# Attention and a gated feed-forward layer on one core: long-run loads with an on-chip permutation, a new order of loads, stores and transposes, and weight sums on GpSimd

## The chip, the cores and the metric

The kernel runs on one core of one Trainium2 chip. The metric is the device time of one execution in microseconds (us), as a median of several runs; the kernel before takes 463.4 us. Engines in the profile: PE (matmul), PEld (its weight loads), DVE (VectorE), ACT (ScalarE), POOL (GpSimd), SP (SyncE, which here only issues DMAs). Each engine works through its own queue in the order in which the program was emitted. An engine that waits with nothing else to do is said to "stand". A ratio below is the mean time of one kernel's fast runs over that of the kernel before's fast runs of the same rounds on the same chip, so it is not quite the ratio of the medians that stand beside it. The kernel before itself came out at 460 to 465 us on different occasions; so kernels are compared by ratios, and a difference of 0.01 between two ratios is 4.6 us.

## The reference, cut to what matters

```python
# q, k, v: (8 batches, 12 heads, 448 rows, 64);  w_gate, w_val: (768, 1536);  w_out: (1536, 768); all float32
scores = q @ k.T / sqrt(64)
attn   = maximum(scores, 0) ** 2 / 448
x      = heads of (attn @ v) side by side        # 3584 tokens x 768
out    = (maximum(x @ w_gate, 0) * (x @ w_val)) @ w_out
```

The kernel works in bf16 with float32 accumulation. Four heads of one batch make a "quad"; there are 24 quads, three to a batch.

## The kernel before: the parts that matter

The kernel doesn't emit instructions in the order in which it is written. Every operation is an `Op` with a guessed duration per engine; a planner simulates all engines, picks for each operation engine and time, and emits everything in the order of the planned starts. On the chip that order is fixed, right or wrong: if an input is later than planned, the engine stands at that instruction, and all behind it stand too (in the kernel before, DVE stood 10.62 us at one instruction whose weights landed at 104.6 us, and did 0.63 us of work between 92.8 and 104.4).

```python
        op.start, op.eng = s, e
        self.t[e] = s + occ                                    # engine free again
        op.end = s + busy                                      # result there
        if op.load:
            self.dmaq = max(self.dmaq, s + occ + 1.0) + op.load
            op.end = self.dmaq + 1.0                           # guessed landing of a load
        op.end += op.land                                      # the same for transposes and stores
```

Q and k of batches 2 to 7 are loaded in runs of 64 elements straight into the layout that the crossbar wants (`raw`, one buffer), four DMAs a quad, and transposed by DMA, five transposes a quad (a "crossbar group" below):

```python
    src = lambda x: x[b, hs].rearrange("h (p t) d -> p t h d", t=NT)
    ...
    op = Op({"SP": (0.2, 0.2)}, emit, deps=st.qk_ops, alloc=[st.qt_buf], reads=[st.raw_buf])   # five DMA transposes
    op.land = 5.0
```

Batches 2 to 7 use Strassen's scheme for two batches at a time: seven products in place of eight. For that, twelve sums of weights (128x1536 bf16) are formed once, in place, when the plain feed-forward of batches 0 and 1 is done:

```python
    def make_T(after):
        for g in range(KH):
            prev = []
            for o, a, c in (...):                              # four a group, each after the one ahead of it
                op = Op({"DVE": (0.85, 0.97)}, lambda ...: nc.vector.tensor_tensor(
                    o(g), a(g), c(g), ALU.subtract), deps=after + prev)
```

Other two-input work of DVE: the squares (`at*at`), the sums of x (`sx`, `xT`) and of h (`sh`) for Strassen. They read both inputs from SBUF.

Of the kernel before, what the change touches and what calls it, by code (L numbers as in the profile page):

```python
# [53 lines left out]
class Planner:  # L54
    NOUT = 8
    SWITCH = 0.1

    def __init__(self):
        self.t = {}
# [18 lines left out]
    def best(self, op):  # L78
        r = self.ready(op)
        if r is None:  # L80
            return None
        c = None
        for e, (occ, busy) in op.engs.items():
            s = max(r, self.t.get(e, 0.0))
            if e == "PE" and op.mode != self.mode:
                s = max(r, self.t.get(e, 0.0) + self.SWITCH)
            if c is None or s + busy < c[0]:
                c = (s + busy, s, e)
        return c[1], c[2], r

    def commit(self, op, s, e):
        op.start, op.eng = s, e
        occ, busy = op.engs[e]
        self.t[e] = s + occ
        op.end = s + busy
        if e == "PE":
            self.mode = op.mode
        if op.load:
            self.dmaq = max(self.dmaq, s + occ + 1.0) + op.load
            op.end = self.dmaq + 1.0  # L100
            self.landed.append(op.end)
        op.end += op.land
        for b in op.alloc:
            b.idx = b.pick()[1]
            for w in range(b.width):
                del b.res.free[b.idx + w]
            b.last = op.end
        for b in op.reads:
            b.readers -= 1
            b.last = max(b.last, op.end)  # L110
            if b.readers == 0:
                for w in range(b.width):
                    b.res.free[b.idx + w] = b.last
        self.ops.append(op)


def plan(att, ffn, others, pool, deadline):
# [16 lines left out]
    while ai < len(att) or fi < len(ffn) or active or pi < len(pool):  # L134
        cands = []
        for op in active:
            b = P.best(op)
            if b is not None:
                cands.append((b[0], b[2], 1, b[1], op))
        if pi < len(pool):  # L140
            b = P.best(pool[pi])
            if b is not None:
                s = b[0]
                if pi >= P.NOUT:
                    s = max(s, P.landed[pi - P.NOUT])
                cands.append((s, 0.0, 0, "POOL", pool[pi]))
        A = P.best(att[ai][0]) if ai < len(att) else None
        F = P.best(ffn[fi][0]) if fi < len(ffn) else None
        pick = None
        if ai < len(att) and fi < len(ffn) and last_grp is not None and last_grp == ffn[fi][0].grp:  # L150
            pick = "F" if F is not None else None
        elif A is not None and F is not None:
            if att[ai][1] == last_burst:
                pick = "A" if A[0] <= F[0] + 0.4 else "F"
            elif since >= gap:
                pick = "A" if A[0] <= F[0] + 0.15 else "F"
            else:
                pick = "F" if F[0] <= A[0] + 0.3 else "A"
        elif A is not None:
            pick = "A"  # L160
        elif F is not None:
            pick = "F"
        if pick == "A":
            cands.append((A[0], A[2], 2, "PE", att[ai][0]))
        elif pick == "F":
            cands.append((F[0], F[2], 2, "PE", ffn[fi][0]))
        assert cands, f"no operation can start: {ai} {fi} {len(active)} {pi}"
        s, _, kind, e, op = min(cands, key=lambda c: c[:3])
        P.commit(op, s, e)
        for o in outs.get(id(op), ()):  # L170
            o.missing -= 1
            if not o.missing:
                active.append(o)
        if kind == 0:
            pi += 1
        elif kind == 1:
            active.remove(op)
        elif pick == "A":
            if att[ai][1] != last_burst:
                last_burst = att[ai][1]  # L180
                since = 0.0
            ai += 1
            last_grp = None
            sg = ffn[fi][1] if fi < len(ffn) else None
            left = deadline(sg) - last_burst + 1 if sg is not None and deadline(sg) is not None else 0
            gap = left_work[sg] / max(1, left) if left > 0 else 0.0
        else:
            since += op.engs["PE"][0]
            left_work[ffn[fi][1]] -= op.engs["PE"][0]
            last_grp = op.grp  # L190
            fi += 1
# [5 lines left out]
def kernel(  # L197
# [35 lines left out]
    pool = ctx.enter_context(tc.tile_pool(name="sb", bufs=1))  # L233
    psum = ctx.enter_context(tc.tile_pool(name="psum", bufs=1, space=bass.MemoryType.PSUM))

    N_QT, N_AT, N_X, N_F, N_G, N_O = 3, 11, 3, 5, 4, 6
    N_RAW, N_VV = 1, 3

    ps = psum.tile([128, 8, 512], FP32, name="ps")
    ps_b = ps.bitcast(BF16)  # L240
# [4 lines left out]
    wo = pool.tile([128, 2, 2, FH, OH], BF16, name="wo")  # L245
    gvT = pool.tile([128, 3, KH, d_ff], BF16, name="gvT")
    woT = pool.tile([128, 3, FH, OH], BF16, name="woT")
    raw_t = [pool.tile([128, 2, NT, 2, D], BF16, name=f"raw{i}") for i in range(N_RAW)]
    vv_t = [pool.tile([128, 4, NC + 2, D], BF16, name=f"vv{i}") for i in range(N_VV)]
    qkT_t = [pool.tile([128, 2, 2, S], BF16, name=f"qkT{i}") for i in range(N_QT)]  # L250
    at_t = [pool.tile([128, 2, S], BF16, name=f"at{i}") for i in range(N_AT)]
# [6 lines left out]
    o_t = [pool.tile([128, OH], FP32, name=f"o{i}") for i in range(N_O)]  # L258

    r_ps = Res(8)  # L260
    r_raw, r_vv, r_qt, r_at = Res(N_RAW), Res(N_VV), Res(N_QT), Res(N_AT)
    r_x, r_f, r_g, r_o = Res(N_X), Res(N_F), Res(N_G), Res(N_O)
    r_sx, r_sh, r_h = Res(1), [Res(1) for _ in range(4)], Res(1)

# [7 lines left out]
    A384, V384 = (0.40, 0.54), (0.467, 0.61)  # L272
    A896, V896 = (0.83, 0.98), (1.0, 1.13)

    PAIRS = [0, 2]
    SINGLES = [7, 6, 5, 4]

    def bank(among=None):
# [2 lines left out]
    def bank2(among=None):  # L281
        return Buf(r_ps, among if among is not None else PAIRS, width=2)

# [52 lines left out]

    def load_qk(b, g):
        st = quads[(b, g)] = Quad()
        if b < NPE:
            hs = slice(4 * g, 4 * g + 4)  # L340
            st.raw_buf = None
            st.raw = lambda: early_raw(b, g)
            src = lambda x: x[b, hs].rearrange("h (p t) d -> p h t d", t=NT)
            k_op = dma_in(lambda: st.raw()[64:128], src(k), 256, 1.2)
            q_op = dma_in(lambda: st.raw()[0:64], src(q), 256, 1.2)
            st.qk_ops = [k_op, q_op]
        else:
            st.raw_buf = Buf(r_raw)
            st.raw = lambda: raw_t[st.raw_buf.idx]
            st.qk_ops = []  # L350
            for j in range(2):
                hs = slice(4 * g + 2 * j, 4 * g + 2 * j + 2)
                src = lambda x: x[b, hs].rearrange("h (p t) d -> p t h d", t=NT)
                st.qk_ops += [dma_in(lambda j=j: st.raw()[64:128, j], src(k), 896, 0.9,
                                     alloc=[st.raw_buf] if j == 0 else []),
                              dma_in(lambda j=j: st.raw()[0:64, j], src(q), 896, 0.9)]

    def load_v(b, g):
        st = quads[(b, g)]
# [4 lines left out]
        else:  # L364
# [1 line left out]
            st.vv = lambda: vv_t[st.vv_buf.idx]  # L366
        src = v[b, hs].rearrange("h (p t) d -> p h t d", t=NT)
        st.v_of = lambda hh, c: st.vv()[:, hh, 1 + c, :]
        v0 = dma_in(lambda: st.vv()[0:64, :, 1:NC + 2], src[:, :, 0:NC + 1], 256, 0.7,
                    alloc=[st.vv_buf] if st.vv_buf else [])  # L370
        v1 = dma_in(lambda: st.vv()[64:128, :, 0:NC + 1], src[:, :, NC:NT], 256, 0.7)
        st.v_ops = [v0, v1]


    def transpose_pe(b, g):
        st = quads[(b, g)]
        ps2 = bank2()

        def emit():
            raw = st.raw()  # L380
# [27 lines left out]
    def transpose_dma(b, g):  # L408
        st = quads[(b, g)]
        st.qt_buf = Buf(r_qt)  # L410

        def emit():
            raw, qkT = st.raw(), qkT_t[st.qt_buf.idx]
            nc.sync.dma_start_transpose(out=qkT[:, 0].rearrange("p j (t c) -> p (j t) c", c=P2),
                                        in_=raw[0:64].rearrange("p j t h d -> p (j t h d)"))
            for j in range(2):
# [1 line left out]
                for o, t0, t1 in ((0, 0, NC + 1), (1, NC + 1, NT)):  # L418
                    nc.sync.dma_start_transpose(out=kT[:, o:NT:2], in_=raw[64:128, j, t0:t1].rearrange("p t h d -> p (t h d)"))  # L419

        op = Op({"SP": (0.2, 0.2)}, emit, deps=st.qk_ops, alloc=[st.qt_buf], reads=[st.raw_buf])
        op.land = 5.0
        st.qt_ops = [op]
        others.append(op)

    xop, xbuf = {}, {}

    class Attention:
# [11 lines left out]
            return qkT_t[self.st.qt_buf.idx][64 * h2:64 * h2 + 64, 1, j, o:o + n]  # L440

        def s(self, i):
            ps2 = bank2()
            tail = i == 2 * NC
            at = self.at[i] = Buf(r_at)

# [28 lines left out]

        def pv(self):
            b, g, st = self.b, self.g, self.st
            ps2 = bank2()

            def emit_tail():  # L480
                at = at_t[self.at[2 * NC].idx]
# [79 lines left out]
    def make_T(after):  # L561

        res = {}
        for g in range(KH):
            prev = []
            for o, a, c in ((lambda g: gvT[:, 1, g], lambda g: wv[:, 2 * g + 1], lambda g: wv[:, 2 * g]),
                            (lambda g: wv[:, 2 * g], lambda g: wv[:, 2 * g], lambda g: wg[:, 2 * g]),
                            (lambda g: gvT[:, 0, g], lambda g: wv[:, 2 * g + 1], lambda g: wv[:, 2 * g]),
                            (lambda g: gvT[:, 2, g], lambda g: wg[:, 2 * g + 1], lambda g: gvT[:, 0, g])):
                op = Op({"DVE": (0.85, 0.97)}, lambda o=o, a=a, c=c, g=g: nc.vector.tensor_tensor(  # L570
                    o(g), a(g), c(g), ALU.subtract), deps=after + prev)
                others.append(op)
                prev = [op]
# [137 lines left out]
    def store(ob, op, where):  # L711
# [4 lines left out]
            for half, (bb, t) in enumerate(slots):  # L716
                nc.sync.dma_start(out=rows(bb)[t][:, hf * OH:(hf + 1) * OH], in_=o_t[ob.idx][64 * half:64 * half + 64])

        st = Op({"SP": (0.15, 0.15)}, emit, deps=[op], reads=[ob])
        st.land = 2.5  # L720
        others.append(st)

# [91 lines left out]
        load_v(0, g)  # L814
    for c in range(d_ff // WC):
        load_gv(c)
        if c % 2 == 0:
            load_qk(1, c // 2)
            load_v(1, c // 2)
    for g in range(NQ):  # L820
        load_qk(2, g)
        load_v(2, g)
        if g > 0:
            load_out(0, g - 1)
    load_out(1, 0)
    load_out(1, 1)
    for b in range(3, B):
        for g in range(NQ):
            load_qk(b, g)
# [22 lines left out]
    for n, qd in enumerate(A_):  # L852
# [1 line left out]
        att += [(qd.s(0), burst), (qd.s(1), burst)]  # L854
        burst += 1
        att.append((qd.s(2 * NC), burst))
        PV(n - 1)
        T(n + 1)
        burst += 1
        att += [(qd.s(2), burst), (qd.s(3), burst)]  # L860
        burst += 1
        att += [(qd.s(4), burst), (qd.s(5), burst)]
    burst += 1
    PV(len(A_) - 1)

# [45 lines left out]
```

## Time and profile before

| | before |
|---|---|
| median of runs | 463.4 us |
| PE busy, of 464.7 us | 415.1 us |
| DVE busy | 332.8 us |
| feed-forward begins | 43.5 us |
| DVE stands at the output weights | 10.6 us |
| POOL waits for the crossbar to free `raw` | 126.7 us |

PE is the bound on average, and the question is only where its 50 idle microseconds lie and what they wait for. The prediction below shows the lines and reads them.

### The profile page before, as it was taken

How to read it: one execution, taken by the hardware profiler on the slowest of the kernel's cores; microseconds unless marked ns; L12 is line 12 of the kernel's file. 1: busy time of each engine (PE TensorE's matmuls, PEld its weight loads, DVE VectorE, ACT ScalarE, POOL GpSimd, SP SyncE). 2: the span in 40 equal slices, each digit the busy share in tenths (PEclk: the TensorE clock that was granted, in tenths of full speed). 3: DMA queues.
4: the chain of work that ended last, by engine and by line, in shares of the span. 5: the costliest groups of instructions: out<-in, count | busy, mean ns of one | idle time of the engine just before them, and what ended most of it. 6: DMA issues, size and time to landing. Idle time of an engine off the chain costs nothing.

```text
span 464.7 us, 7076 instructions
## 1 busy us (share of the span) xinstructions
PE 415.1 (89%) x2580; PEld 195.2 (42%) x2580; DVE 332.8 (72%) x576; ACT 221.9 (48%) x329; POOL 134.9 (29%) x154
## 2 busy tenths in 40 slices
PE   4768999968988948799999978999999999999994
PEld 2333444423433413244444443444444555555552
DVE  3665877709798833788979967988889686666561
ACT  2564555553574522456555434665654634444221
POOL 7745150605533353145333442253200000000000
PEclk9977999997997968799999999999999999999999
DMA  9999989999857996998669898996721332000144
GB/s 128 196 198 198 151 70 100 108 147 79 82 59 87 122 132 92 128 155 70 74 82 90 85 118 147 167 83 68 72 27 27 76 86 52 1 0 2 34 103 102
DMA packets 138659, 44.13 MB, mean 95 GB/s; under 512 B 103808, under 2 KB 138624, under 8 KB 138624
## 3 DMA queue, kind: packets, MB, share of 16 engines
q0 software_dynamic: 94528, 24.39, 54.5%
q1 hardware_dynamic: 44096, 19.29, 20.9%
q8 instruction: 20, 0.33, 0.3%
q14 instruction: 15, 0.12, 0.1%
HBM read 48.76 MB, written 11.01 MB: 129 GB/s over the span
## 4 chain that ended last, share of the span: by engine, by line
PE 71%; DMA 9%; DVE 7%; SPq 4%; ACT 4%; issue 3%; POOL 1%; DVEq 0%; POOLq 0%; ACTq 0%
PE ps L643 29%; PE ps L744 17%; PE ps L544 8%; PE ps L493 6%; PE ps L451 6%; DMA wo<-in_moe_w_out_dram 4%; SPq L419 3%; DMA out_dram<-o 3%; ACT at L465 3%; PE ps L384 2%; DVE at L467 1%; DMA qkT<-raw 1%; DVE at L470 1%; PE ps L455 1%; PE ps L485 1%
## 5 line engine op out<-in xcount | busy, mean ns | idle before, releaser
L465 ACT ACTIVATE at<-ps 128x896 bf16<-128x896 f32 x117 | 104.4, 918 | 69.2 <-PE ps L451 55.3
L470 DVE TENSOR_TENSOR at<-at 128x896 bf16<-128x896 bf16 x168 | 99.7, 618 | 13.5 <-ACT at L465 13.4
L592 ACT COPY f<-ps 128x448 f32<-128x448 f32 x105 | 55.8, 533 | 66.4 <-PE ps L643 64.5
L288 POOL DMA_DIRECT2D raw<-in_k_dram x36 | 46.2, 1284 | 141.0 <-DMA qkT<-raw 126.7
L467 DVE TENSOR_SCALAR at<-ps 128x896 bf16<-128x896 f32 x51 | 55.3, 1085 | 6.9 <-PE ps L451 6.7
L288 POOL DMA_DIRECT2D raw<-in_q_dram x36 | 59.7, 1662 | 0.3 <-DMA wv<-in_moe_w_val_dram 0.3
L643 PE MATMUL ps<-xT,gvT 128*128 128x448 bf16 x216 | 53.3, 356 | 2.6 <-DVE o L734 2.5
L643 PE MATMUL ps<-sx,wv 128*128 128x448 bf16 x216 | 52.8, 353 | 1.7 <-DVE g L662 1.1
L451 PE MATMUL ps<-qkT 64*128 64x448 bf16 x288 | 45.5, 379 | 9.8 <-ACT at L465 7.1
L643 PE MATMUL ps<-xT,wg 128*128 128x448 bf16 x216 | 52.8, 356 | 0.5 <-DVE g L700 0.5
L288 POOL DMA_DIRECT2D vv<-in_v_dram x44 | 36.4, 1044 | 47.5 <-PE ps L493 40.4
L643 PEld LDWEIGHTS <-gvT 128*128 128x128 bf16 x324 | 31.1, 98 | 37.1 <-issue 9.9
L734 DVE SCALAR_TENSOR_TENSOR o<-ps,f 128x384 f32<-128x384 f32 x40 | 22.0, 554 | 31.1 <-DMA out_dram<-o 16.0
L744 PE MATMUL ps<-wo,hT 128*128 128x384 bf16 x240 | 43.8, 326 | 0.2 <-DVE hT L666 0.2
L744 PEld LDWEIGHTS <-sh 128*128 128x128 bf16 x288 | 27.9, 101 | 36.2 <-issue 10.8
L744 PEld LDWEIGHTS <-hT 128*128 128x128 bf16 x312 | 30.1, 99 | 24.6 <-issue 5.8
L744 PE MATMUL ps<-woT,sh 128*128 128x384 bf16 x144 | 30.1, 359 | 8.4 <-DVE sh L781 8.3
L544 PE MATMUL ps<-xT,wv 128*128 128x448 bf16 x144 | 32.3, 362 | 5.8 <-DVE hT L554 5.8
L493 PE MATMUL ps<-at,vv 128*64 128x448 bf16 x264 | 33.2, 393 | 0.0
L544 PE MATMUL ps<-xT,wg 128*128 128x448 bf16 x144 | 32.6, 364 | 0.0
L594 ACT ACTIVATE f<-ps 128x384 f32<-128x384 f32 x40 | 19.6, 491 | 27.2 <-PE ps L744 26.0
L508 ACT CAST xT<-ps 128x896 bf16<-128x896 f32 x24 | 21.7, 905 | 19.4 <-PE ps L493 19.4
(56 smaller groups left out, 442.1 us busy)
## 6 DMA issues: line engine op xcount, KB each, us to landing
out_dram<-o SPq DMA_DIRECT2D x112, 96.0 KB, 2.9
vv<-in_v_dram POOLq DMA_DIRECT2D x44, 128.0 KB, 5.2
raw<-in_k_dram POOLq DMA_DIRECT2D x36, 112.0 KB, 3.9
raw<-in_q_dram POOLq DMA_DIRECT2D x36, 112.0 KB, 5.0
wg<-in_moe_w_gate_dram POOLq DMA_DIRECT2D x6, 384.0 KB, 11.3
wv<-in_moe_w_val_dram POOLq DMA_DIRECT2D x6, 384.0 KB, 11.2
wo<-in_moe_w_out_dram POOLq DMA_DIRECT2D x4, 576.0 KB, 13.2
qkT<-raw SPq DMA_TRANSPOSE x90, 3.2
```

The source lines that it names most:

```text
L288: op = Op({"POOL": (0.5 + 0.0004 * n_desc,) * 2}, lambda: nc.gpsimd.dma_start(out=dst(), in_=src), deps=deps, alloc=alloc)
L451: nc.tensor.matmul(ps[:, ps2.idx + h2, :S], lhsT=self.k_of(j, h2, c), rhs=self.q_of(j, h2), start=True, stop=True)
L465: nc.scalar.activation(at_t[at.idx], src, AF.Relu)
L467: nc.vector.tensor_scalar_max(at_t[at.idx], src, 0.0)
L470: sq = Op({"DVE": (0.535, 0.66)}, lambda: nc.vector.tensor_tensor(at_t[at.idx], at_t[at.idx], at_t[at.idx], ALU.mult), deps=[relu])
L493: nc.tensor.matmul(ps[o, ps2.idx + j, :S], lhsT=st.v_of(2 * j + h2, c), rhs=at_t[self.at[NC * j + c].idx][:, h2, :], start=False, stop=(c ...
L508: nc.scalar.copy(dst, src)
L544: nc.tensor.matmul(ps[:, pb.idx, :S], lhsT=w[:, kd, fc], rhs=xT_t[xbuf[b].idx][:, kd, :], start=(kd == 0), stop=(kd == KD - 1))
L592: nc.scalar.copy(dst, src)
L643: nc.tensor.matmul(ps[:, pb.idx, :S], lhsT=w(g)[:, fc], rhs=rhs, start=start and g == 0, stop=stop and g == KH - 1, skip_group_check=True)
L734: op = Op({"DVE": V384}, lambda: nc.vector.scalar_tensor_tensor(o_t[ob.idx], ps[:, pb.idx, :OH], float(out_scale), f_t[fb.idx][:, :OH], AL ...
L744: nc.tensor.matmul(ps[:, pb.idx, :OH], lhsT=lhs(kf), rhs=rhs(kf), start=start and kf == 0, stop=kf == FH - 1, skip_group_check=True)
```

## The change

Its intent: longer DMA runs and fewer DMA issues; `raw` freed early by a permutation on chip, so that loads run ahead of the crossbar; a plan that knows what SP's queue really costs; output weights earlier; a denser start; and twelve weight sums taken off busy DVE onto idle GpSimd. The core of the diff, cuts marked "...":

```diff
-            self.dmaq = max(self.dmaq, s + occ + 1.0) + op.load
-            op.end = self.dmaq + 1.0
+            self.dmaq = max(self.dmaq, s + occ + 0.3) + op.load
+            op.end = self.dmaq + 2.0
...
-    N_QT, N_AT, N_X, N_F, N_G, N_O = 3, 11, 3, 5, 4, 6
+    N_QT, N_AT, N_X, N_F, N_G, N_O = 3, 10, 3, 5, 4, 5
...
-    PAIRS = [0, 2]
+    PAIRS, FIRST_PAIRS = [0, 2], [0, 2, 4, 6]            # FIRST_PAIRS: for batch 0
...
+        hs = slice(4 * g, 4 * g + 4)                     # all batches: two DMAs a quad, long runs
+        src = lambda x: x[b, hs].rearrange("h (p t) d -> p h t d", t=NT)
...
+        perm = Op({"DVE": (0.6, 0.72), "ACT": (1.8, 1.95)}, None, deps=st.qk_ops, alloc=[pb], reads=[st.raw_buf])
+        ...      src = st.raw()[:, 2 * j:2 * j + 2].rearrange("p h t d -> p t h d")
+        ...      nc.vector.tensor_copy(dst, src)          # j = 0, 1; dst = perm_t[pb.idx][:, j]
-        op = Op({"SP": (0.2, 0.2)}, emit, deps=st.qk_ops, alloc=[st.qt_buf], reads=[st.raw_buf])
-        op.land = 5.0
+        op = Op({"SP": (6.3, 6.3)}, emit, deps=[perm], alloc=[st.qt_buf], reads=[pb])
+        op.land = 2.6
...
-                op = Op({"DVE": (0.85, 0.97)}, lambda ...: nc.vector.tensor_tensor(
+                op = Op({"POOL": (2.8, 2.9)}, lambda ...: nc.gpsimd.tensor_tensor(
...
-        st = Op({"SP": (0.15, 0.15)}, emit, deps=[op], reads=[ob])      # a pair of stores
+        st = Op({"SP": (1.2, 1.2)}, emit, deps=[op], reads=[ob])
... (guessed load times changed a little; output weights ahead of the second quad of batch 2; q, k, v of batch 1 one weight chunk later;
     the product of quad 2 and the transposes of quad 3 moved ahead of quad 3's scores;
     0.3 us of bias towards ACT where DVE and ACT can both do an operation)
```

More of the change, by code (lines that the diff above doesn't have):

```diff
@@ L56 @@
     SWITCH = 0.1
+    BIAS = 0.3
+    RESERVE = 0.0
     def __init__(self):
@@ L86, in best @@
                 s = max(r, self.t.get(e, 0.0) + self.SWITCH)
-            if c is None or s + busy < c[0]:
-                c = (s + busy, s, e)
+            f = s + busy + (self.BIAS if e == "DVE" and len(op.engs) > 1 else 0.0)
+            if c is None or f < c[0]:
+                c = (f, s, e)
         return c[1], c[2], r
@@ L185, in plan @@
             left = deadline(sg) - last_burst + 1 if sg is not None and deadline(sg) is not None else 0
-            gap = left_work[sg] / max(1, left) if left > 0 else 0.0
+            gap = max(0.0, left_work[sg] - P.RESERVE) / max(1, left) if left > 0 else 0.0
         else:
@@ L234 @@
     psum = ctx.enter_context(tc.tile_pool(name="psum", bufs=1, space=bass.MemoryType.PSUM))
-    N_QT, N_AT, N_X, N_F, N_G, N_O = 3, 11, 3, 5, 4, 6
-    N_RAW, N_VV = 1, 3
+    N_QT, N_AT, N_X, N_F, N_G, N_O = 3, 10, 3, 5, 4, 5
+    N_RAW, N_PERM, N_VV = 1, 1, 3
     ps = psum.tile([128, 8, 512], FP32, name="ps")
@@ L247 @@
     woT = pool.tile([128, 3, FH, OH], BF16, name="woT")
-    raw_t = [pool.tile([128, 2, NT, 2, D], BF16, name=f"raw{i}") for i in range(N_RAW)]
+    raw_t = [pool.tile([128, 4, NT, D], BF16, name=f"raw{i}") for i in range(N_RAW)]
+    perm_t = [pool.tile([128, 2, NT, 2, D], BF16, name=f"perm{i}") for i in range(N_PERM)]
     vv_t = [pool.tile([128, 4, NC + 2, D], BF16, name=f"vv{i}") for i in range(N_VV)]
@@ L260 @@
     r_ps = Res(8)
-    r_raw, r_vv, r_qt, r_at = Res(N_RAW), Res(N_VV), Res(N_QT), Res(N_AT)
+    r_raw, r_perm, r_vv, r_qt, r_at = Res(N_RAW), Res(N_PERM), Res(N_VV), Res(N_QT), Res(N_AT)
     r_x, r_f, r_g, r_o = Res(N_X), Res(N_F), Res(N_G), Res(N_O)
@@ L338, in load_qk @@
         st = quads[(b, g)] = Quad()
-        if b < NPE:
-            hs = slice(4 * g, 4 * g + 4)
-            st.raw_buf = None
-            st.raw = lambda: early_raw(b, g)
-            src = lambda x: x[b, hs].rearrange("h (p t) d -> p h t d", t=NT)
-            k_op = dma_in(lambda: st.raw()[64:128], src(k), 256, 1.2)
-            q_op = dma_in(lambda: st.raw()[0:64], src(q), 256, 1.2)
-            st.qk_ops = [k_op, q_op]
-        else:
-            st.raw_buf = Buf(r_raw)
-            st.raw = lambda: raw_t[st.raw_buf.idx]
-            st.qk_ops = []
-            for j in range(2):
-                hs = slice(4 * g + 2 * j, 4 * g + 2 * j + 2)
-                src = lambda x: x[b, hs].rearrange("h (p t) d -> p t h d", t=NT)
-                st.qk_ops += [dma_in(lambda j=j: st.raw()[64:128, j], src(k), 896, 0.9,
-                                     alloc=[st.raw_buf] if j == 0 else []),
-                              dma_in(lambda j=j: st.raw()[0:64, j], src(q), 896, 0.9)]
+        hs = slice(4 * g, 4 * g + 4)
+        st.raw_buf = None if b < NPE else Buf(r_raw)
+        st.raw = lambda: early_raw(b, g) if b < NPE else raw_t[st.raw_buf.idx]
+        src = lambda x: x[b, hs].rearrange("h (p t) d -> p h t d", t=NT)
+        k_op = dma_in(lambda: st.raw()[64:128], src(k), 256, 1.15, alloc=[st.raw_buf] if b >= NPE else [])
+        q_op = dma_in(lambda: st.raw()[0:64], src(q), 256, 1.15)
+        st.qk_ops = [k_op, q_op]
     def load_v(b, g):
@@ L368, in load_v @@
         st.v_of = lambda hh, c: st.vv()[:, hh, 1 + c, :]
-        v0 = dma_in(lambda: st.vv()[0:64, :, 1:NC + 2], src[:, :, 0:NC + 1], 256, 0.7,
+        v0 = dma_in(lambda: st.vv()[0:64, :, 1:NC + 2], src[:, :, 0:NC + 1], 256, 0.66,
                     alloc=[st.vv_buf] if st.vv_buf else [])
-        v1 = dma_in(lambda: st.vv()[64:128, :, 0:NC + 1], src[:, :, NC:NT], 256, 0.7)
+        v1 = dma_in(lambda: st.vv()[64:128, :, 0:NC + 1], src[:, :, NC:NT], 256, 0.66)
         st.v_ops = [v0, v1]
@@ L376, in transpose_pe @@
         st = quads[(b, g)]
-        ps2 = bank2()
+        ps2 = bank2(FIRST_PAIRS if b == 0 else PAIRS)
         def emit():
@@ L410, in transpose_dma, with emit_perm @@
         st.qt_buf = Buf(r_qt)
+        pb = Buf(r_perm)
+        perm = Op({"DVE": (0.6, 0.72), "ACT": (1.8, 1.95)}, None, deps=st.qk_ops, alloc=[pb], reads=[st.raw_buf])
+        def emit_perm():
+            for j in range(2):
+                dst = perm_t[pb.idx][:, j]
+                src = st.raw()[:, 2 * j:2 * j + 2].rearrange("p h t d -> p t h d")
+                if perm.eng == "ACT":
+                    nc.scalar.copy(dst, src)
+                else:
+                    nc.vector.tensor_copy(dst, src)
+        perm.emit = emit_perm
         def emit():
-            raw, qkT = st.raw(), qkT_t[st.qt_buf.idx]
+            raw, qkT = perm_t[pb.idx], qkT_t[st.qt_buf.idx]
             nc.sync.dma_start_transpose(out=qkT[:, 0].rearrange("p j (t c) -> p (j t) c", c=P2),
@@ L419, in emit @@
                     nc.sync.dma_start_transpose(out=kT[:, o:NT:2], in_=raw[64:128, j, t0:t1].rearrange("p t h d -> p (t h d)"))
-        op = Op({"SP": (0.2, 0.2)}, emit, deps=st.qk_ops, alloc=[st.qt_buf], reads=[st.raw_buf])
-        op.land = 5.0
+        op = Op({"SP": (6.3, 6.3)}, emit, deps=[perm], alloc=[st.qt_buf], reads=[pb])
+        op.land = 2.6
         st.qt_ops = [op]
-        others.append(op)
+        others.extend([perm, op])
     xop, xbuf = {}, {}
@@ L442, in s @@
         def s(self, i):
-            ps2 = bank2()
+            ps2 = bank2(FIRST_PAIRS if self.b == 0 else PAIRS)
             tail = i == 2 * NC
@@ L477, in pv @@
             b, g, st = self.b, self.g, self.st
-            ps2 = bank2()
+            ps2 = bank2(FIRST_PAIRS if b == 0 else PAIRS)
             def emit_tail():
@@ L569, in make_T @@
                             (lambda g: gvT[:, 2, g], lambda g: wg[:, 2 * g + 1], lambda g: gvT[:, 0, g])):
-                op = Op({"DVE": (0.85, 0.97)}, lambda o=o, a=a, c=c, g=g: nc.vector.tensor_tensor(
+                op = Op({"POOL": (2.8, 2.9)}, lambda o=o, a=a, c=c, g=g: nc.gpsimd.tensor_tensor(
                     o(g), a(g), c(g), ALU.subtract), deps=after + prev)
@@ L816 @@
         load_gv(c)
-        if c % 2 == 0:
+        if c % 2 == 1:
             load_qk(1, c // 2)
             load_v(1, c // 2)
-    for g in range(NQ):
-        load_qk(2, g)
-        load_v(2, g)
-        if g > 0:
-            load_out(0, g - 1)
-    load_out(1, 0)
-    load_out(1, 1)
+    load_qk(2, 0)
+    load_v(2, 0)
+    for par in range(2):
+        for hf in range(2):
+            load_out(par, hf)
+        load_qk(2, 1 + par)
+        load_v(2, 1 + par)
     for b in range(3, B):
@@ L856 @@
         att.append((qd.s(2 * NC), burst))
-        PV(n - 1)
-        T(n + 1)
+        if n != NQ:
+            PV(n - 1)
+        if n != NQ - 1:
+            T(n + 1)
         burst += 1
@@ L862 @@
         att += [(qd.s(4), burst), (qd.s(5), burst)]
+        if n == NQ - 1:
+            burst += 1
+            PV(n)
+            T(n + 1)
     burst += 1
```

## The prediction

> **What bounds the kernel now.** I read the page first (busy shares, slices), then the stretches of 11.6 us, then the chain of waits, the waits by engine, and the timelines of PE, DVE, POOL and the DMA queue of SP.
>
> ```profile
> PE 415.1 (89%) x2580; PEld 195.2 (42%) x2580; DVE 332.8 (72%) x576; ACT 221.9 (48%) x329; POOL 134.9 (29%) x154
> ...
> PEclk9977999997997968799999999999999999999999
> ```
>
> PE is the bound on average, yet it is idle for 464.7 - 415.1 = about 50 us, and the low figures of the PEclk row all lie in the first 17 slices (about 197 us). The stretches say where:
>
> ```profile
> 23.20:34.80 11.60, 7.65 (x64) 3.60 (x63) 7.03 (x12) 7.00 (x8) 5.77 (x9) 0.71 1.42 197
> 46.40:58.00 11.60, 11.60 (x99) 5.64 (x98) 10.24 (x16) 6.20 (x8) 2.34 (x3) 1.00 1.42 152
> 92.80:104.40 11.60, 8.00 (x50) 3.39 (x47) 0.63 (x2) 6.33 (x9) 0.00 (x0) 1.00 1.29 149
> 162.40:174.00 11.60, 4.95 (x22) 1.95 (x22) 3.64 (x8) 3.13 (x6) 5.89 (x6) 0.68 0.98 126
> ```
>
> After the window come its length, then PE, PEld, DVE, ACT and POOL busy time, granted clock, DMA share and GB/s. Where attention runs beside the feed-forward part (second row) PE is full. Summing 11.6 minus PE busy over all stretches: 0 to 46 us loses 15.5; 81 to 116 loses 6.5; 127 to 151 loses 3.2; 162 to 197 loses 11.2; 266 to 290 loses 4.2; the drain of the last tiles 5.5; everything else about 3. That is 49. So only about 40 us are up for discussion, four fifths of them ahead of 197 us; from there to 440 us PE is 98% busy and no change off PE can help much.
>
> Each gap has a second price. The timeline shows the same six plain 448-column matmuls at 1.30 us in most of the run and at 2.40 us at 106.6, right after a gap. Clock 0.71 in a stretch is, at half rate while cold, 0.58 x 11.6 = 6.7 cold us, in which work takes double time: up to 3.3 us more per such stretch. Behind the later gaps (104 to 116, 139 to 151, 162 to 197) I estimate 10 to 12 us of this, and before 43 us everything is cold: the 12 matmuls of one attention product take 2.4 us, later 1.26.
>
> The chain and the waits name the causes:
>
> ```profile
> 72.36 1.54 SPq L419
> 73.95 6.16 DMA qkT<-raw
> ...
> 86.59 18.02 DMA wo<-in_moe_w_out_dram
> ...
> 166.37 3.63 DMA out_dram<-o
> ...
> 183.78 3.69 DMA out_dram<-o
> ...
> 275.88 5.08 DMA out_dram<-o
> ```
> ```profile
> POOL raw L288 <- DMA qkT<-raw: 126.7, 19, 16.1
> ...
> DVE o L734 <- DMA out_dram<-o: 16.0, 4, 7.1
> ...
> DVE woT L583 <- DMA wo<-in_moe_w_out_dram: 10.6, 1, 10.6
> ```
>
> (waited us in total, times, longest). First, DVE stands 10.6 us in its queue at the output-weight sum because the last output weights land at 104.6; PE runs out of evicted banks 5.8 us before that ends. Second, stores stand behind transposes in SP's queue: at 159.0 to 165.7 SP issues one crossbar group (five transposes, 1.24 us each, 6.3 in all), the six output tiles fill, DVE waits 7.07 us and PE 6.5; the same at 182 and 273. Third, q and k loads wait for the previous crossbar group, since there is one raw buffer: the groups start at 113.7, 129.1, 143.5, 159.0, 174.0, 190.7, one in about 15 us. Fourth, in the first 43 us each quad costs 10.3 us, because only two pairs of PSUM banks take scores: PE waits for a ReLU, one burst at a time.
>
> **What the Trainium skill says.** "TensorE: Matmul & The Clock Gate", Part 1: an idle PE falls to 1.2 GHz and needs some 3.4 us of sustained work to come back; the trace agrees (2.40 against 1.30 us). "SBUF — State Buffer", Who interferes with whom: GpSimd shares a port pair with DVE, and a DVE instruction with two SBUF inputs and a GpSimd one that reads SBUF exclude each other for a whole instruction. The kernel before has no GpSimd arithmetic beside DVE work, so no run shows it yet. "GPSIMD Engine Reference", section 3.1: two-input element-wise work at about 2.6 cycles per element; for 1536 columns at 1.2 GHz that gives an estimate of 3.3 us against 0.95 us measured here on DVE. "DMA: Bandwidth & Descriptors", Specifications: below 512 B a transfer loses rate; here 103808 of 138659 packets are under 512 B.
>
> **The change part by part.**
> *Long runs.* Four POOL DMA issues per quad with 256-byte source runs become two with 1792-byte runs. Now 72 issues, (46.2 + 59.7) / 72 = 1.47 us each, 106 us of POOL; the same form exists for the first two batches at 0.64 us, so 36 x 0.64 = 23 us after. POOL is not on the path; this saves 83 us of room there, and some load on the DMA engines.
> *Permutation.* 18 quads x 2 copies of 128x896 bf16. As DVE copies from SBUF I expect 0.3 to 0.4 us each, 18 x 0.7 = 13 us on DVE. It releases the raw buffer early, so the next load overlaps this crossbar group. Cycle per quad: before, load about 5 + issue 6.3 + landing 3.2 = 14.5 (the trace shows 15); after, about 6.3 + 3.2 + 0.7 = 10. Attention of batches 2 and 3 can be complete some 20 us earlier, so PE has other work in hand in 160 to 197.
> *Weight sums on GpSimd.* Off DVE: 12 x 0.95 = 11.3 us in one chain at 131 to 140, which roughly pays for the permutation. On POOL: 12 x about 3 = 36 us, starting when the plain feed-forward ends (about 120) and needed when the first Strassen stage starts (about 170): fits, with some 14 us of slack. The 3.2 us gap and its cold tail go; but squares (0.62 us) and sums of DVE in that stretch can be held up to 3 us each. I take +3 net.
> *Output weights earlier, planner with real SP times, landings 1 us later.* The 10.6 us DVE stand goes: 6 us of PE idle plus 3 us of cold clock, +9.
> *Stores ordered with SP's 6.3 us known.* The plan now sees transposes and stores (1.2 us a pair) in one queue. The queue itself is as full as before: in an output stage 14 pairs x 1.2 = 17 us plus two or three groups, in about 35 us; and there are five output tiles instead of six. Of the 15 us of store gaps (6.5, 4.5, 4.2) with 6 us of cold clock I take a little over half: +11.
> *Start.* Four bank pairs for batch 0. A quad needs 7 ReLUs of about 1 us, 7 squares of 0.62, one copy of 0.9, two of 0.62: 13.5 us over two engines, 6.8 each; PE, cold, needs about 7.2 dense. So about 7.7 a quad instead of 10.3, three quads: -8. Moving the product of quad 2 ahead of quad 3's scores moves work, no time. +8.
> *Losses.* Permutation in DVE's strict order waiting for a late load or crossbar, ten score buffers instead of eleven: -2.
>
> Sum: 9 + 11 + 3 + 8 - 2 = 29. 463.4 - 29 = 434; rounded up a little for what a static plan misses: **435 us**.
>
> **Rivals.** (a) *The store queue stays the bound.* Same 6.3 us blocks, fewer tiles; for it: chain pieces at 166, 184 and 276 are all stores. Then the +11 shrinks to about 3: 443. (b) *GpSimd sums become the wait*: 12 instructions stretched to 4 to 5 us by port exclusion, 50 to 60 us, end near 180; the first Strassen stage waits, and DVE squares stall meanwhile. Against: DVE is idle often enough at that stage. It would cost 5 to 12 us: 440 to 447. (c) *DVE stands at the permutation* as it stood at the output weights, because now a compute engine waits for a DMA (landings reach 13 us at 46 to 60 us). One microsecond for each of 18 quads, half of it hidden: 9 us. (d) *All hidden*: PE 98% busy from 197 on means attention done earlier only swaps order. It does bound the gain: removing every gap and all cold work gives 464.7 - 50 + 12 (unavoidable start and drain) - 12 - about 10 cold at start, about 405. (e) Better: a denser start also warms the clock early and all store gaps go, 420.
>
> **Range.** Gains add up from five independent places, of which the output weights and the start are nearly certain (17 us, already 446); the others pull between 420 and 450. So 421 to 450, faster 0.93, within 2% (454 to 473) 0.06, slower 0.01.
>
> **What would show each step.** Right: no wait of DVE for output weights; PE idle before 43 us down to about 8 and feed-forward starting near 34 us; PE idle in 160 to 197 under 5; crossbar groups about 10 us apart where loads are the limit; POOL raw waits for a crossbar replaced by short ones; GpSimd sums near 3 us and over before the first Strassen product that reads them. Wrong: a large wait on the permutation's load, on GpSimd sums, or again on stores; GpSimd sums far over 3 us with squares near them stretched beyond 0.62; scores of batch 0 still one burst per 1.4 us. What would make the number wrong most: a new gap of PE in 100 to 200 us that I do not foresee, with its cold clock.

## The result, and the profile after

The changed kernel takes 482.8 us (479.9 to 488.9, four runs, one of them slow) against 463.35: ratio 1.040, with a 95% interval of 1.035 to 1.045. It is slower by 4%, where 6% faster was foretold.

Busy shares and granted clock on its page, in the form already shown of the kernel before:

```profile
PE 411.9 (86%) x2580; PEld 194.4 (40%) x2580; DVE 360.5 (75%) x581; ACT 235.6 (49%) x348; POOL 109.8 (23%) x130
...
PEclk9989996799958597999999999999999999999999
```

PE does the same work in slightly less time, but DVE is 28 us busier although sums were taken from it. Next, stretches of 11.6 us of the changed kernel (columns as in the prediction):

```profile
69.60:81.20 11.60, 7.04 (x36) 2.61 (x36) 9.08 (x14) 5.50 (x7) 1.25 (x2) 0.80 1.41 159
127.60:139.20 11.60, 4.34 (x28) 2.09 (x25) 11.60 (x2) 2.98 (x5) 11.60 (x5) 0.80 0.48 60
150.80:162.40 11.60, 5.43 (x36) 2.41 (x32) 10.80 (x5) 5.12 (x7) 10.94 (x7) 0.83 0.70 122
174.00:185.60 11.60, 3.48 (x22) 1.51 (x21) 11.53 (x5) 3.09 (x5) 10.55 (x6) 0.86 0.89 144
```

In three of them DVE is "busy" nearly throughout with 2 to 5 instructions, POOL is busy too, and PE is idle for 6 to 8 us. The timeline of POOL and of DVE in the changed kernel (start, length, engine, line, operation; "x3" means three in a row):

```profile
126.24 9.21 POOL L577 TENSOR_TENSOR gvT<-wv 128x1536 bf16<-128x1536 bf16 x3
135.38 6.14 POOL L577 TENSOR_TENSOR wv<-wv,wg 128x1536 bf16<-128x1536 bf16 x2
```
```profile
126.53 1.08 DVE L474 TENSOR_SCALAR at<-ps 128x896 bf16<-128x896 f32 x1
127.53 14.41 DVE L788 TENSOR_TENSOR sh<-hT 128x768 bf16<-128x768 bf16 x1
141.87 1.15 DVE L477 TENSOR_TENSOR at<-at 128x896 bf16<-128x896 bf16 x2
142.94 0.54 DVE L788 TENSOR_TENSOR sh<-hT 128x768 bf16<-128x768 bf16 x1
...
153.37 10.00 DVE L630 TENSOR_TENSOR xT<-xT,xT 128x448 bf16<-128x448 bf16 x1
...
174.69 10.29 DVE L788 TENSOR_TENSOR sh<-hT,sh 128x768 bf16<-128x768 bf16 x1
```

An instruction that takes 0.54 us took 14.41: it began among five GpSimd sums issued back to back and ended at 141.9, just after the fifth (141.5). The twelve sums come in four rows, of five, three, three and one, and each holds one DVE instruction with two SBUF inputs: 14.41, 10.00, 10.29 and 3.43 us, 36 us over their normal 0.4 to 0.6. The ReLU at 126.53 reads PSUM only; it ran in its normal 1.08 us although a sum had started at 126.24. PE waits right behind the first three (its timeline; in brackets the wait before the instruction and what ended it):

```profile
143.54 2.10 PE L751 MATMUL ps<-woT,sh 128*128 128x384 bf16 x6 [11.60 <-DVE sh L788]
163.90 4.02 PE L751 MATMUL ps<-woT,sh 128*128 128x384 bf16 x12 [7.67 <-DVE sh L788]
186.33 0.56 PE L458 MATMUL ps<-qkT 64*128 64x448 bf16 x2 [8.85 <-DVE at L474]
```

That is 28 us of PE in three waits. This is one suspect. The second is in the waits of the changed kernel (waited us in total, times, longest):

```profile
DVE perm L415 <- DMA qkT<-perm: 9.7, 4, 5.1
DVE perm L415 <- issue: 5.5, 6, 1.9
DVE perm L415 <- DMA raw<-in_q_dram: 2.6, 2, 1.3
...
DVE woT L590 <- DMA wo<-in_moe_w_out_dram: 0.8, 1, 0.8
```

The stand at the output weights is gone (0.8 us, before 10.6), but DVE now stands 17.8 us in all ahead of the permutation.

### The profile page after: what moved, and what is told of

Its sections match the earlier page's. It is cut to its first block, busy times and chain, and to the rows that moved or that the text cites. A ratio compares the mean times of both kernels' runs of the same rounds, so it can differ in the third digit from the quotient of the medians.

```text
span 481.6 us, 7040 instructions
## 1 busy us (share of the span) xinstructions
PE 411.9 (86%) x2580; PEld 194.4 (40%) x2580; DVE 360.5 (75%) x581; ACT 235.6 (49%) x348; POOL 109.8 (23%) x130
## 2 busy tenths in 40 slices
DMA packets 82785, 44.11 MB, mean 92 GB/s; under 512 B 38720, under 2 KB 82752, under 8 KB 82752
## 4 chain that ended last, share of the span: by engine, by line
PE 52%; DMA 20%; DVE 16%; issue 4%; SPq 3%; POOL 3%; ACT 2%; DVEq 0%; ACTq 0%; POOLq 0%
PE ps L650 20%; PE ps L751 14%; PE ps L551 8%; DMA qkT<-perm 6%; DVE sh L788 6%; DMA gvT<-in_q_dram 5%; PE ps L500 4%; DMA raw<-in_q_dram 4%; PE ps L458 3%; DVE xT L630 2%; SPq L426 2%; DVE at L477 2%; DMA gvT<-in_k_dram 1%; DMA out_dram<-o 1%; DVE at L474 1%
## 5 line engine op out<-in xcount | busy, mean ns | idle before, releaser
L472 ACT ACTIVATE at<-ps 128x896 bf16<-128x896 f32 x125 | 110.5, 924 | 57.3 <-PE ps L458 46.7
L477 DVE TENSOR_TENSOR at<-at 128x896 bf16<-128x896 bf16 x168 | 98.2, 616 | 7.1 <-ACT at L472 6.9
L292 POOL DMA_DIRECT2D vv<-in_v_dram x44 | 27.2, 628 | 212.0 <-PE ps L500 202.8
L474 DVE TENSOR_SCALAR at<-ps 128x896 bf16<-128x896 f32 x43 | 46.6, 1083 | 14.8 <-PE ps L458 14.7
L415 DVE COPY perm<-raw 128x896 bf16<-128x896 bf16 x34 | 19.5, 612 | 17.9 <-DMA qkT<-perm 9.7
L551 PE MATMUL ps<-xT,wg 128*128 128x448 bf16 x144 | 32.7, 365 | 0.0
L650 PEld LDWEIGHTS <-wg 128*128 128x128 bf16 x216 | 20.3, 98 | 25.7 <-issue 8.2
## 6 DMA issues: line engine op xcount, KB each, us to landing
wo<-in_moe_w_out_dram POOLq DMA_DIRECT2D x4, 576.0 KB, 12.9
```

Of the source, the lines that this page charges most:

```text
L292: op = Op({"POOL": (0.5 + 0.0004 * n_desc,) * 2}, lambda: nc.gpsimd.dma_start(out=dst(), in_=src), deps=deps, alloc=alloc)
L472: nc.scalar.activation(at_t[at.idx], src, AF.Relu)
L474: nc.vector.tensor_scalar_max(at_t[at.idx], src, 0.0)
L477: sq = Op({"DVE": (0.535, 0.66)}, lambda: nc.vector.tensor_tensor(at_t[at.idx], at_t[at.idx], at_t[at.idx], ALU.mult), deps=[relu])
L551: nc.tensor.matmul(ps[:, pb.idx, :S], lhsT=w[:, kd, fc], rhs=xT_t[xbuf[b].idx][:, kd, :], start=(kd == 0), stop=(kd == KD - 1))
L650: nc.tensor.matmul(ps[:, pb.idx, :S], lhsT=w(g)[:, fc], rhs=rhs, start=start and g == 0, stop=stop and g == KH - 1, skip_group_check=True)
```

## The experiments

**Theory 1**: a GpSimd sum excludes DVE's two-SBUF-input instructions. **Theory 2**: DVE, which works strictly in order, stands at the permutation because the plan puts it earlier than loads and crossbar really land. **Theory 3**: the smaller buffers (five output tiles, ten score tiles) and the new store order cost it. Fourteen kernels ran, all correct (the record has no e9); each ratio is to the kernel before.

### e1: sums back on DVE

```diff
-                op = Op({"POOL": (2.8, 2.9)}, ... nc.gpsimd.tensor_tensor(
+                op = Op({"DVE": (0.85, 0.97)}, ... nc.vector.tensor_tensor(
```

> The changed kernel with one thing undone: the twelve weight sums back on DVE (planned at 0.85 us). Theory 1 (a GpSimd sum holds DVE's two-input instructions out; four DVE instructions of 14.41, 10.00, 10.29 and 3.43 us in the changed kernel, 36 us over their normal 0.4 to 0.6): no DVE instruction over 2 us, PE idle between 127 and 200 us down from about 31 us to under 12, time 440 to 455. Theory 2 (the permutation in DVE's order waits for loads and the crossbar): 470 to 483, since 11 us of sums come back to DVE. Theory 3 (new plan with five output tiles and ten score tiles): 470 to 483.

464.3 us, ratio 1.009 (0.999 to 1.018). No DVE instruction is held any more, PE's idle time from 127.6 to 197 us falls from 28.1 to 11.1 us, and theory 1 accounts for 0.031, or 14 us. But the result lies outside the range that theory 1 gave: with the exclusion gone, the change is still no gain. The rows of this kernel's groups for the permutation (count, busy us, mean ns, idle before and its releasers) show the next suspect:

```profile
L415 DVE COPY perm<-raw 128x896 bf16<-128x896 bf16 x34 | 19.6, 614 | 30.4 <-issue 15.3 <-DMA raw<-in_q_dram 7.7 <-DMA qkT<-perm 7.5
L413 ACT COPY perm<-raw 128x896 bf16<-128x896 bf16 x2 | 1.8, 936 | 2.3 <-DMA qkT<-perm 2.3
```

("issue" stands for a wait whose releaser the profile doesn't show.) Engines stand 32.7 us ahead of the permutation, more than the 17.8 of the changed kernel. PE stands shortly after: from 50 us on it has nine waits of over 1 us, 19.8 us in all, and each ends 1.7 to 2.8 us after the start of a permutation at which an engine had stood. Two of them:

```profile
177.09 1.15 DVE L415 COPY perm<-raw 128x896 bf16<-128x896 bf16 x2 [2.71 <-DMA raw<-in_q_dram]
179.81 0.73 PE L650 MATMUL ps<-sx,wv 128*128 128x448 bf16 x3 [3.34 <-DVE g L669]
...
287.29 1.14 DVE L415 COPY perm<-raw 128x896 bf16<-128x896 bf16 x2 [3.68 <-issue]
289.02 0.73 PE L650 MATMUL ps<-xT,wg 128*128 128x448 bf16 x3 [2.69 <-DVE g L707]
```

### e2: the kernel before, sums on GpSimd

The opposite edit in the kernel before.

> The kernel before with one thing done: the twelve weight sums on GpSimd. Theory 1: single DVE instructions of 6 to 15 us appear between 127 and 200 us, time 480 to 500. Theories 2 and 3: 11 us less on DVE, 455 to 464.

491.0 us, ratio 1.068 (1.060 to 1.076). Four rows of three sums, four held instructions (the first line is two instructions, one of them held); the timeline of DVE:

```profile
135.21 12.36 DVE L470 TENSOR_TENSOR at<-at 128x896 bf16<-128x896 bf16 x2
...
152.58 9.99 DVE L623 TENSOR_TENSOR sx<-xT 128x448 bf16<-128x448 bf16 x1 [1.93 <-ACT xT L508]
...
177.05 10.10 DVE L623 TENSOR_TENSOR xT<-xT,xT 128x448 bf16<-128x448 bf16 x1
...
198.56 10.00 DVE L623 TENSOR_TENSOR sx<-xT 128x448 bf16<-128x448 bf16 x1 [0.80 <-ACT xT L508]
```

Theory 1 is shown in both directions: this one edit costs 7% by itself.

### e3: sums on GpSimd, but never two in a row

```diff
+                tick = Op({"DVE": (0.1, 0.15)}, lambda o=o, g=g: nc.vector.tensor_copy(z[:, 0:1], o(g)[:, 0:1]), deps=[op])
+                tock = Op({"POOL": (0.1, 0.15)}, lambda: nc.gpsimd.tensor_copy(z[:, 1:2], z[:, 0:1]), deps=[tick])
```

> The changed kernel, with a one-column DVE copy and a one-column GpSimd copy between every two GpSimd sums, so that GpSimd can't start the next sum before DVE has run on. Theory 1: no DVE instruction is held longer than one sum, about 3.1 us; the sums spread out; time 458 to 475. If the holding is not tied to back-to-back sums: still instructions of 9 us and over, time 480 or more. Theories 2 and 3: 482.

471.6 us, ratio 1.025 (1.016 to 1.034). The profiled run was one of the slow ones (475.2 us), so only the instruction lengths are read from it. The longest single two-input instructions of DVE there:

```profile
144.81 3.44 DVE L794 TENSOR_TENSOR sh<-hT 128x768 bf16<-128x768 bf16 x1
...
150.70 3.64 DVE L478 TENSOR_TENSOR at<-at 128x896 bf16<-128x896 bf16 x1
```

With a DVE instruction forced between sums, an instruction is held for about one sum (3.1 us) at most, and the ratio falls from 1.040 to 1.025, 7 us. So the holds of 10 to 14 us come from sums that follow each other without a break, as theory 1 expected.

### e4: no permutation, sums on GpSimd

Loads in short runs straight into the permuted layout, as before the change; the rest as changed.

> The changed kernel with q and k loaded in short runs straight into the permuted layout, and no permutation; sums stay on GpSimd. Theory 1: the DVE stalls at the sums stay, 475 to 490. Theory 2: 455 to 466.

476.3 us, ratio 1.036 (1.027 to 1.046). With the sums on GpSimd the time hardly changes without the permutation. It is no clean removal, though: DVE instructions are held 14.2, 17.6 and 12.2 us there, longer than in the changed kernel. The question was open again with the sums on DVE.

### e5: sums on DVE and no permutation

e1 and e4 together.

> The changed kernel with sums on DVE (as in e1) and also without the permutation (short runs as before): what is left is the new start, the earlier output weights and the new plan. Theory A (with the sums back on DVE, the permutation standing in DVE's strict order costs what the start and the output weights gain: DVE idle ahead of the permutation is 30 us in e1): 446 to 456. Theory B (output tiles five, score tiles ten and the new store order cost it): 459 to 466, like e1.

441.6 us, ratio 0.955 (0.950 to 0.960): 25 us under e1, and better than even theory A had expected. Five output tiles, ten score tiles and the new store order are all still in it, so theory 3 falls: they don't keep the kernel from gaining. What each costs or gains by itself was not tested.

### e6: sums on DVE, plan told later landings

```diff
-            op.end = self.dmaq + 2.0
+            op.end = self.dmaq + 5.0
...
-        op.land = 2.6
+        op.land = 5.0
```

> e1 with the plan alone told more time: loads land 5.0 instead of 2.0 us after their transfer, crossbar groups 5.0 instead of 2.6. So DVE's copies are placed later in its order. Theory A: waits of DVE at the permutation fall from 30 us to under 12, time 448 to 458. Theory B: waits fall too, but the time stays 459 to 466.

439.2 us, ratio 0.949 (0.945 to 0.954), the fastest of all (e14 below is level with it) and below the range of theory A. Two numbers in the plan, which change the order and the choice between DVE and ACT but no instruction's work, give 0.059, or 27 us. The row of the permutation and the page's first lines for this kernel:

```profile
L415 DVE COPY perm<-raw 128x896 bf16<-128x896 bf16 x34 | 19.4, 610 | 6.7 <-DMA qkT<-perm 4.6 <-DMA raw<-in_q_dram 2.1
```
```profile
PE 401.2 (92%) x2580; PEld 191.3 (44%) x2580; DVE 335.9 (77%) x595; ACT 233.5 (53%) x346; POOL 72.9 (17%) x118
...
PEclk9989999799999999999999999999999999999999
```

The standing fell from 32.7 to 6.7 us, and after the first four slices the PEclk row has one slice under 9 (in the changed kernel six).

### e7: v loads behind the next quad's q and k

```diff
+    late = [(b, g) for b in range(3, B) for g in range(NQ)]
+    for n, (b, g) in enumerate(late):
+        load_qk(b, g)
+        if n > 0:
+            load_v(*late[n - 1])
+    load_v(*late[-1])
```

On e1. This puts q and k ahead of v from batch 3 on (the text of the expectation names an earlier quad; the edit is as shown).

> e1 with the v load of a quad issued behind the q and k loads of the next, from the third quad of batch 2 on; in e1 q and k stand behind v, and v waits for a product (190 us of waits on GpSimd's queue). Theory A, with late q and k loads as the cause: DVE's waits for q and k loads vanish, 450 to 459. Otherwise 460 to 466.

449.0 us, ratio 0.973 (0.966 to 0.981), just under the range of theory A. The waits put down to late q and k loads fell from 7.7 to 1.3 us, and the 15.3 us without a shown releaser went; the wait for the crossbar is 16.5 us (9.8 in e1, of DVE and ACT). About half of the standing is left (17.8 us), and six tenths of e6's gain is reached.

### e8 and e10: the two gains that were held nearly certain, alone

e8 is the kernel before with the four bank pairs and the new order at the start; e10 has the earlier output weights as well.

> The kernel before with the new start alone: four bank pairs for batch 0 and the product of quad 2 moved ahead of quad 3. As predicted (8 us, or 12 as the profile of the changed kernel shows the feed-forward starting at 31 us and not 43): 451 to 456. If the gain is given back further on, at the output weights that land at 104 us whatever PE does: 459 to 463.

460.2 us, ratio 0.994 (0.988 to 1.000). The feed-forward begins at 29.9 us and not at 43.5, and yet almost nothing comes of it. One wait of DVE, and one of PE behind it, took nearly all:

```profile
DVE woT L583 <- DMA wo<-in_moe_w_out_dram: 19.0, 1, 19.0
...
PE ps L544 <- DVE hT L554: 14.2, 1, 14.2
```

The output weights land at 105 us whatever PE does; whoever comes there earlier waits longer: 19.0 in place of 10.6 us on DVE, 14.2 in place of 5.8 on PE.

> The kernel before with the new start and the output weights loaded earlier. In e8 the start alone made the feed-forward begin at 30 us instead of 43.5, and DVE then stood 19.0 us instead of 10.6 at the output weights. If that is where the start's gain went: DVE's stand falls below 5 us, time 443 to 450 (the 17 us of the prediction for both). If the gain is lost elsewhere: 455 to 462.

456.1 us, ratio 0.995 (0.987 to 1.002): in the range for a gain lost elsewhere, and not at the 446 of the prediction. The condition of the test, a stand of DVE below 5 us, was not met either: the weights are there at 83.7 us and DVE comes still earlier. PE behind it waits only 2.2 us now, but further on it waits more:

```profile
DVE woT L583 <- DMA wo<-in_moe_w_out_dram: 12.9, 1, 12.9
...
PE ps L744 <- DVE o L734: 7.5, 1, 7.5
...
PE ps L744 <- DVE sh L781: 6.3, 1, 6.3
PE ps L451 <- DMA qkT<-raw: 4.6, 1, 4.6
```

The waits for `sh` and `o` end at 163 and 181 us, where DVE itself stands 6.84 and 9.71 us at output tiles whose stores are queued behind crossbar groups on SP (the chain has SP's issues, then 3.4 and 4.3 us of output DMA); the last, at 84 us, is for a crossbar group itself. What was gained at the front is lost at the queue that comes next.

### e11, e12, e13: the other corners

e11 is the changed kernel, sums on GpSimd, with e6's landings; e12 is e6 with e7's loads; e13 is e5 with both of e6's edits.

> The changed kernel, sums still on GpSimd, with the later landings of e6 in the plan: the fourth corner of sums (GpSimd, DVE) by landings (changed, later). If both causes add: 482.8 + 439.2 - 464.3 = 458, within 452 to 464, with DVE instructions of about 10 us still there. If the exclusion hides the late landings: 465 to 480.

471.3 us, ratio 1.030 (1.020 to 1.040), above the range for adding causes. The four corners, as ratios: changed landings with sums on GpSimd 1.040, on DVE 1.009; later landings with sums on GpSimd 1.030, on DVE 0.949. Each cause hides part of the other: with the sums on GpSimd the later landings cut the standing from 17.8 to 6.9 us, and the time by only 0.010, 5 us, with intervals that overlap.

> e6 (sums on DVE, later landings) with e7's v loads behind the next quad's q and k. If e6 has removed nearly all standing of DVE at the permutation, nothing is left for e7: 436 to 441. If late q and k loads still cost: 430 to 436.

439.7 us, ratio 0.959 (0.952 to 0.966): nothing over e6. Standing 8.7 us.

> e5 (sums on DVE, no permutation) with the later landings. Tells whether the permutation itself gains anything once no engine stands at it. If long runs and the permutation gain by earlier q and k: 440 to 446, slower than e6. If not: 434 to 440.

477.1 us, ratio 1.042 (1.033 to 1.051), far outside both ranges. PE waits 20.0 us at three crossbar groups:

```profile
PE ps L455 <- DMA qkT<-raw: 20.0, 3, 8.6
```

On SP, 14 store issues (14.9 us from 126.3) stand ahead of one of its crossbar groups and 10 more (7.7 us) ahead of the next, for which PE waits 8.6 us until 162.4. So the same landings that help with the permutation hurt without it: a change of order alone cost 40 us here (e13 against e5), and this raised the doubt that e6 had only met a lucky one. Why the plan of e13 orders SP's queue so was not followed further.

### e14 and e15: standing, or luck?

e14 is e1 with the permutation alone planned 3 us later, all landings as in the change; e15 has landings half way between e1 and e6.

```diff
-            r = max(r, d.end)
+            r = max(r, d.end + op.lag)         # and the same for its buffer
...
+        perm.emit, perm.lag = emit_perm, 3.0
```

> e1 with one thing changed in the plan: the permutation alone is planned 3 us after its inputs and its buffer are planned to be free; every other landing stays as in the change. If DVE (and in e1 two ACT copies) standing at the permutation is the cause: standing under 15 us of 30, time 438 to 450. If e6's gain came from other moves of the plan: 458 to 466.

442.3 us, ratio 0.950 (0.943 to 0.958). Permutation in this kernel:

```profile
L415 DVE COPY perm<-raw 128x896 bf16<-128x896 bf16 x32 | 18.3, 613 | 5.6 <-DMA qkT<-perm 3.5 <-DMA raw<-in_q_dram 2.1
```

> e6 half way: loads land 3.5 us and crossbar groups 3.8 us after. If the standing at the permutation is the cause, time and standing both lie between e1 (464, 30 us) and e6 (439, 5 us): 440 to 458. If the time only follows accidents of the order: outside that.

449.4 us, ratio 0.964 (0.958 to 0.970). With the sums on DVE and the permutation in place, in order of standing (DVE and ACT together, from each kernel's groups):

| kernel | standing at the permutation, us | ratio to before |
|---|---|---|
| e1 | 32.7 | 1.009 |
| e7 | 17.8 | 0.973 |
| e15 | 10.9 | 0.964 |
| e12 | 8.7 | 0.959 |
| e6 | 6.7 | 0.949 |
| e14 | 5.6 | 0.950 |

Six plans, two of them made from e1 without touching a landing (e7 and e14): the time falls with the standing, about 1 us for each. And where PE has nine waits of over 1 us in e1 after 50 us, it has two in e14 (1.75 and 1.02). Theory 2 is shown for this kernel with the sums on DVE; each new plan also moves other work, and e13 warns that this is not always harmless.

Where PE's time went, busy us of PE in three stretches (from the windows of each profile):

| stretch, length | before | changed | e1 | e6 |
|---|---|---|---|---|
| 69.6 to 92.8, 23.2 | 22.5 | 16.2 | 16.9 | 17.5 |
| 127.6 to 197, 69.4 | 55.0 | 41.3 | 58.3 | 63.1 |
| 197 to 266, 69.0 | 68.2 | 60.7 | 63.5 | 66.6 |

The second row is where the GpSimd sums sit; e1 gets 17 us back there. In the third the changed kernel and e1 lose 5 to 7 us that the kernel before doesn't, and e6 gets most of them back (the changed kernel has one last sum there). The first stays low in e6 too, and in e10, which has no permutation (15.4). In e6 4.3 of the 5.7 idle us are waits for ReLUs that DVE does late, after standing 4.6 us at two permutations; in e10 4.6 of 7.8 are the crossbar group at 84 us and 2.2 follow DVE's stand at the output weights.

## Why the prediction was wrong

- **The GpSimd step failed, in sign.** The prediction put it at "+3 net", with DVE instructions "held up to 3 us each", and its rival (b) at 5 to 12 us. That the engines exclude each other had been read correctly; for how long had not. The sums took 3.07 us each (9.21 / 3), near enough, but GpSimd ran them in rows, and one DVE instruction waits for the whole row: 36 us of holding in four pieces. It costs 14 us of time beside the landings of the change (1.040 against 1.009) and 37 where those are mended (1.030 against 0.949). "DVE is idle often enough at that stage" was the wrong argument against it: in the kernel before DVE is busy 30.6 of the 34.8 us from 127.6 to 162.4, and a held instruction also holds what stands behind it in DVE's queue and PE waits for (the three waits of 11.60, 7.67 and 8.85 us above).
- **The loss term "-2" for the permutation was too small.** Rival (c) named it at 9 us. With the sums on DVE, taking the standing in e1 down to that in e6 is worth 27 us, over ten times the term; in the changed kernel, where the sums hide most of it, about 5 us (e11). The copies too were dearer: 0.61 us in place of 0.3 to 0.4, 21 us in all for the expected 13.
- **"Start: +8" and "+9" for the output weights did not add.** As events both were right: the feed-forward began at 31.7 us (34 foretold), and DVE's stand at the output weights fell to 0.8. But PE's idle time before 43.5 us fell only from 15.5 to 12.9 us, not to 8. ("Before 43 us everything is cold" doesn't fit the prediction's own clock row, which is at 9 for the first 23 us.) As a gain they failed: e8 and e10, with both in the kernel before, moved the time by under 1%, not clear of noise, for the saved time was spent at the next late arrival. Together with the rest of the plan they can pay: e5, without permutation, is 21 us faster than the kernel before (ratio 0.955).
- **"+11" for the stores** was not measured by itself. The waits of DVE and ACT for output tiles fell from 29.7 us to 12.1, as meant. e5 shows that start, output weights, stores and plan together are worth 21 us of the 28 that these three terms gave.
- **Long runs and the permutation** did most of what they were meant to do, and no gain is shown for it. Packets under 512 B fell from 103808 to 38720, and POOL's issues of q and k loads from 106 to 23 us, as foretold. The crossbar groups from 72 to 120 us start 12 us apart in the changed kernel (10 foretold, 15 before), and by 200 us e6 has begun eleven of them where e5, without permutation, has begun nine. Yet e6 and e5, whose plans differ in the landings too, are only 0.006 apart, with intervals that overlap: that is what rival (d), "all hidden", says. In e1 and in the changed kernel the loads of q and k stood behind v loads on GpSimd's queue, and these waited for products:

```profile
POOL vv L292 <- PE ps L500: 202.8, 15, 23.3
```

This is the changed kernel; the wait for the crossbar (126.7 us before) was replaced by one for v's buffers.

So two faults in the change, one an engine choice and one two constants of the plan, make the 42 us between the changed kernel and e6 (1.040 and 0.949). That e6 comes within 1% of the foretold 435 us doesn't confirm the sum: e6 has the "+3" undone and the plan retuned, "+8" and "+9" did not add, and "+11" was not measured. The 0.3 us of bias and the later loads of batch 1 were not tested alone.

## What to carry to other kernels

Before moving element-wise work to an idle GpSimd, look whether DVE has two-SBUF-input work at the same time; if so, the row of GpSimd instructions is what it waits for, not one. Where a plan fixes the order, try placing an instruction that waits for a DMA later on its engine rather than earlier: planned three microseconds later, the permutation alone gained 6% here (e14 against e1). Later landings in general are no such rule (e13 lost by them). And gains ahead of a common late arrival don't add; look for the next wait before adding them up.

## What the Trainium skill lacked or had wrong

- "SBUF — State Buffer", Who interferes with whom, says that whoever issues first holds the shared pair for the whole instruction. What it lacks: a row of GpSimd instructions without a break holds DVE for the row. Measured: 14.41 us behind five sums of 3.07 us, 9.99 to 10.29 behind three, 3.4 to 3.6 where the sums were kept apart. Nor did the first start decide by the trace's times: three of the four held DVE instructions of the changed kernel start 0.04 to 0.65 us before the first sum of their row (starts on GpSimd are rough in this profile).
- "GPSIMD Engine Reference", section 3.1: its measured times are for float32, and it has none for bf16. Its 2.6 cycles per element gave an estimate of 3.3 us for 1536 columns; measured 3.07 us in bf16, so it served.
- "VectorE: DVE Perf Modes", The perf-mode tier table, lists a bf16 copy from SBUF to SBUF at four times the basic rate, but the page ties that rate to conditions on the operands, so nothing here is shown to be wrong. The permuting copy of 128x896 took 0.61 us against the prediction's 0.3 to 0.4; whether it misses a condition was not checked, and no run shows which part of its pattern costs it.
